# Loading batch 1's q and k ahead of WC1 and placing its first attention steps among batch 0's token steps, with one token-major q,k buffer

## The chip, the cores and the metric

The kernel runs on one core of a Trainium2 chip. The metric is the device time of one execution in microseconds (us); less is better. Of several executions the median is given. A profile is one execution, recorded instruction by instruction; its span runs from the first to the last instruction.

## The reference

What is computed is an attention with a sliding window and a linear bias, followed by an MLP mixer:

```
scores = q @ k^T / sqrt(64);  allowed where 0 <= i - j < 128
attn   = softmax(scores - slope[h] * |i - j|)            # slope[h] = 2 ** -(h + 1)
x      = attn @ v, heads side by side                    # (8, 576, 512)
u      = x + (relu(x^T @ w_tok1) @ w_tok2)^T             # mixing over 576 tokens, 256 hidden
out    = u + relu(u @ w_ch1) @ w_ch2                     # mixing over 512 channels, 1536 hidden
```

There are 8 batches, 8 heads, 576 tokens and a head dimension of 64. Inputs and output are float32; the kernel works in bfloat16 with float32 sums.

## The kernel before, in words

All work is in one program; every engine carries out its own instructions in the order in which they stand in its queue. Heads go in pairs, and a pair of a batch has a number `g`: batch 0 has pairs 0 to 3, batch 1 has 4 to 7, and so on. For each pair there are these steps:

- `regroup` (L139): two DVE copies, one for q and one for k, that bring the raw loads `qn`, `kn` into token-major order, `qg`, `kg`. It is done for a whole batch (in batch 0 for each pair). The raw tiles and the regrouped tiles have two buffers each, by `b % 2`.
- `att_T` (L193): twelve PE transposes of `qg`, `kg` into a PSUM tile `tT`, then a copy of q's half by ACT (L211, `qT`) and of k's half by DVE (L212, `kT`). In batch 0 ACT does both. `qT` and `kT` have four buffers each.
- `att_S` (L214), twice per pair: the score matmuls into `sp` (L230), two exponentials by ACT into `pe` (L238), a multiplication with the mask by DVE into `pb` (L242).
- `att_V` (L248): the matmuls of `pb` with v into `ot` (L264), then reciprocal and multiplication by DVE into `xb` (L271, L272). After the last pair of a batch it issues the loads of v two batches on.

The tiles `tT`, `sp` and `ot` share two PSUM buffers (`ps_at`); all PSUM tiles of the mixer share four (`ps_ma`).

The mixer of a batch goes in these steps: `tok1` twice (L304, matmuls at L307, a relu by ACT at L312), `tok2` five times (L315, matmuls at L320, addition of `xb` into `ub` by DVE at L324), `trans_u` four times (L328, PE transposes at L333 and L337, DVE copy into `UT` at L342), `ch1` 24 times (L344, four matmuls at L348, relu by ACT into `R2` at L353), and `ch2` for four or five chunks in three parts each (L357, matmuls at L376, addition of `ub` by DVE at L388 and a store by SyncE). `mixer_items` (L394) makes a list of these steps for batch `b` with the `ch2` chunks of batch `b - 1` among them, and `spread` (L17) mixes such a list with a list of attention steps, by the costs that are written beside them.

The first block of the body (L434) fixes the order on every engine as written: constants, loads, attention of batch 0, token steps of batch 0, and then `ch1` of batch 0 and the first two `ch2` chunks, mixed with the attention of batch 1. In the second block (L522) only PE's order is fixed as written, and a scheduler orders the other engines.

All loads are issued by POOL (GpSimd), because they convert to bfloat16. They go round eight semaphores, so a load can be issued only when the eighth load before it has landed. In the order of the queue they are: q,k of batch 0 by pairs (L450), v of batch 0, W1 and W2 for the token steps, WC1 in three parts (L463), q,k of batch 1 (L466), WC2 (L467), v of batch 1 (L470 to L472), then q,k of batch 2 (L492), v of batch 2, q,k of batch 3 (L513), and so on. The two iotas from which masks and identity are made (L441, L445) stand behind the first pair of loads.

The regroup of batch 1 stands ahead of batch 1's attention (L511), those of batches 2 and 3 at L517 and L524, and those of batches 4 to 7 in the `ch1` steps of `mixer_items` three batches earlier (L424, L425).

Of the kernel before, what the change touches and what calls it, by code (L numbers as in the profile page):

```python
# [13 lines left out]
TPP = 6  # L14
# [24 lines left out]
def kernel(  # L39
# [11 lines left out]
    nc = tc.nc  # L51
    P = nc.NUM_PARTITIONS
    B, H, S, D = q.shape
# [22 lines left out]

    const = ctx.enter_context(tc.tile_pool(name="const", bufs=1))
    pepool = ctx.enter_context(tc.tile_pool(name="pe", bufs=3))
    pbpool = ctx.enter_context(tc.tile_pool(name="pb", bufs=8))
    xpool = ctx.enter_context(tc.tile_pool(name="xp", bufs=2))  # L80
    rpool = ctx.enter_context(tc.tile_pool(name="rp", bufs=2))
    spool = ctx.enter_context(tc.tile_pool(name="sm", bufs=3))
    upool = ctx.enter_context(tc.tile_pool(name="up", bufs=2))
    opool = ctx.enter_context(tc.tile_pool(name="op", bufs=3))
    ps_at = ctx.enter_context(tc.tile_pool(name="ps_at", bufs=2, space=bass.MemoryType.PSUM))
    ps_ma = ctx.enter_context(tc.tile_pool(name="ps_ma", bufs=4, space=bass.MemoryType.PSUM))


    qn = [const.tile([P, H, TPP * D], bf16, name=f"qn{i}") for i in range(2)]
    kn = [const.tile([P, H, TPP * D], bf16, name=f"kn{i}") for i in range(2)]  # L90
    qg = [const.tile([P, TPP, H, D], bf16, name=f"qg{i}") for i in range(2)]
    kg = [const.tile([P, TPP, H, D], bf16, name=f"kg{i}") for i in range(2)]
    vp = [const.tile([P, NCH, H, D + 1], bf16, name=f"vp{i}") for i in range(2)]
    NR = 4
    qT = [const.tile([P, S], bf16, name=f"qT{i}") for i in range(NR)]
# [43 lines left out]
    def regroup(b, h0, h1, which=(0, 1)):  # L139

        for n in which:
            raw, t = ((qn, qg), (kn, kg))[n]
            nc.vector.tensor_copy(  # L143
                out=t[b % 2][:RP, :, h0:h1, :],
                in_=raw[b % 2][:RP, h0:h1, :].rearrange("p h (j d) -> p j h d", j=TPP),
            )

# [45 lines left out]
    def att_T(g, early=False):  # L193
        b, hp = divmod(g, NHP)
        if early:
            tt = [ps_ma.tile([P, 1024], bf16, name="tT1", tag="ma") for _ in range(2)]
        else:
            t2 = ps_at.tile([P, 2, 1024], bf16, name="tT", tag="at")
            tt = [t2[:, n, :] for n in range(2)]
        for n, t_raw in ((0, qg), (1, kg)):  # L200
            for j in range(TPP):
                nc.tensor.transpose(  # L202
                    tt[n][:, j * RP : (j + 1) * RP],
                    t_raw[b % 2][:RP, j, 2 * hp : 2 * hp + 2, :].rearrange("p h d -> p (h d)"),
                    ident[:RP, :RP],
                )
        def nat(n):
            return tt[n][:, 0:S].rearrange("c (j p) -> c p j", j=TPP)
        def dst(a):
            return a[:, :].rearrange("c (p j) -> c p j", j=TPP)  # L210
        nc.scalar.copy(out=dst(qT[g % NR]), in_=nat(0))  # L211
        (nc.scalar.copy if early else nc.vector.tensor_copy)(out=dst(kT[g % NR]), in_=nat(1))  # L212

    def att_S(g, half):  # L214
        b, hp = divmod(g, NHP)
# [178 lines left out]
    def mixer_items(b, lead=1):  # L394

        chunks = []
        if b > 0:
            cs = list(range(NF)) if (b - 1) % 2 == 0 else [NF] + list(range(NF))
            chunks = [ch2_items(b - 1, c) for c in cs]
        its = []  # L400
        for _ in range(lead if chunks else 0):
            its += chunks.pop(0)
        if b < B:
            its += [(1.07, lambda dh=dh: tok1(b, dh)) for dh in range(NDH)]
            if chunks:
                its += chunks.pop(0)
            mid = chunks.pop(0) if chunks else []
            for c in range(NCH):
                its.append((0.43, lambda c=c: tok2(b, c)))
                if mid and c % 2 == 0:  # L410
                    its.append(mid.pop(0))
            its += mid
            last = chunks.pop() if chunks else []
            for ch in chunks:
                its += ch
            its += last[:1]
            for cb in range(NCB):
                its.append((0.25, lambda cb=cb: trans_u(b, cb)))
            its += last[1:]
            for ht_i in range(NHT):  # L420
                for x in range(2):
                    its.append((0.48, lambda ht_i=ht_i, x=x: ch1(b, ht_i, x)))

                if ht_i in (4, 7) and 0 < b < B - 3:  # L424
                    its.append((0.0, lambda n=ht_i // 7: regroup(b + 3, 0, H, (n,))))  # L425
                if ht_i == 7 and 0 < b < B - 5:
                    its.append((0.0, lambda: dma_qk(b + 5, 0, H)))
        else:
            for ch in chunks:
                its += ch  # L430
        return its


    with tc.manual_schedule():  # L434
        for i in range(2):
            nc.vector.memset(vp[i][:, :, :, D : D + 1], 1.0)
            nc.vector.memset(vp[i][0 : P - TAIL, NF, :, 0:D], 0.0)
        nc.vector.memset(W1[0 : P - TAIL, NF, :], 0.0)
        nc.vector.memset(patT[0 : P - TAIL, :], 0.0)
        dma_qk(0, 0, 2)  # L440
        nc.gpsimd.iota(  # L441
            row[:, :], pattern=[[1, P]], base=0, channel_multiplier=0,
            allow_small_or_imprecise_dtypes=True,
        )
        nc.gpsimd.iota(  # L445
            pidx, pattern=[[0, 1]], base=0, channel_multiplier=1,
            allow_small_or_imprecise_dtypes=True,
        )
        for hp in range(1, NHP):
            dma_qk(0, 2 * hp, 2 * hp + 2)  # L450
        dma_v_tail(0)
        for h in range(H):
            dma_v_head(0, h)
        nc.gpsimd.dma_start(
            out=W1[:, 0:NF, :], in_=moe_w_tok1[0 : NF * P, :].rearrange("(c p) d -> p c d", p=P)
        )
        nc.gpsimd.dma_start(out=W1[P - TAIL : P, NF, :], in_=moe_w_tok1[NF * P : S, :])
        nc.gpsimd.dma_start(
            out=W2[:, :, :], in_=moe_w_tok2.rearrange("(j p) s -> p j s", p=P)
        )  # L460
        for n in range(3):
            cs = slice(n * DCH // 3, (n + 1) * DCH // 3)
            nc.gpsimd.dma_start(  # L463
                out=WC1[:, :, cs], in_=moe_w_ch1[:, cs].rearrange("(j p) h -> p j h", p=P)
            )
        dma_qk(1, 0, H)  # L466
        nc.gpsimd.dma_start(  # L467
            out=WC2[:, :, :], in_=moe_w_ch2.rearrange("(j p) c -> p j c", p=P)
        )
        dma_v_tail(1)  # L470
        for c in range(NF):
            dma_v(1, c)  # L472


        build_consts()
        regroup(0, 0, 2)
        build_bias()
        att_T(0, True)
        build_masks(0)
        regroup(0, 2, 4)  # L480
        att_S(0, 0)
        att_T(1, True)
        build_masks(1)
        att_S(0, 1)
        regroup(0, 4, 6)
        att_S(1, 0)
        att_T(2, True)
        build_masks(2)
        att_S(1, 1)
        regroup(0, 6, 8)  # L490
        if B > 2:
            dma_qk(2, 0, H)  # L492
        att_S(2, 0)
        att_T(3, True)
        build_masks(3)
        att_S(2, 1)
        att_V(0)
        att_S(3, 0)
        att_V(1)
        att_S(3, 1)  # L500
        att_V(2)
        att_V(3)
        nc.vector.tensor_copy(out=swap[:, 0:TAIL], in_=ident[:, TAIL:P])
        nc.vector.tensor_copy(out=swap[:, TAIL:P], in_=ident[:, 0:TAIL])


        its0, its1 = mixer_items(0), mixer_items(1, lead=2)
        n0, n1 = len(its0) - NHT, 6
        for _, f in its0[:n0]:
            f()  # L510
        side = [(0.0, lambda: regroup(1, 0, H))]  # L511
        if B > 3:
            side.append((0.0, lambda: dma_qk(3, 0, H)))  # L513
        for g in range(NHP - 2, 2 * NHP):
            side += att_step(g, NHP, 2 * NHP, outputs=False)
        side += [(0.6, lambda g=g: att_V(g)) for g in range(NHP, 2 * NHP)]
        side.append((0.0, lambda: regroup(2, 0, H)))  # L517
        if B > 4:
            side.append((0.0, lambda: dma_qk(4, 0, H)))
        spread(its0[n0:] + its1[:n1], side)  # L520

    with tc.manual_schedule(engines={ENG.PE}):  # L522
        side = att_step(2 * NHP - 2, 2 * NHP) + att_step(2 * NHP - 1, 2 * NHP)
        side.append((0.0, lambda: regroup(3, 0, H)))  # L524
        if B > 5:
            side.append((0.0, lambda: dma_qk(5, 0, H)))
        for g in range(2 * NHP, 3 * NHP):
            side += att_step(g)
        spread(its1[n1:], side)
        for b in range(2, B + 1):  # L530
            side = []
            for g in range(NHP * (b + 1), NHP * (b + 2)):
                side += att_step(g)
            spread(mixer_items(b), side)
# [30 lines left out]
```

## Time and profile before

| | us |
|---|---|
| median of 3 runs | 346.29 |
| lowest and highest | 345.74, 346.75 |
| the profiled execution | 345.74 |
| its span | 343.9 |
| PE busy in it | 307.2 |
| DVE, ACT, POOL busy in it | 179.6, 178.1, 60.0 |

The profile page begins with busy times, as in the table, and then shows the span in 40 slices of 8.6 us with a digit for the busy tenths of each engine. PE is TensorE, PEld its weight loads, DVE VectorE, ACT ScalarE, POOL GpSimd, SP SyncE. Further views list the groups of instructions by source line, the chain of waits that ended last, the DMA issues with their time to landing, and for any stretch the instructions in order of time. In that last view a line gives start, duration, engine, source line, operation, output and inputs with their sizes, the number of instructions merged into the line, and in brackets the time for which the engine was idle before it, with the releaser. The releaser is inferred, so it can name an instruction that had been done long before.

### The profile page before, as it was taken

What the parts mean: (1) busy time and instruction counts of PE and PEld (TensorE: products, weight loads), DVE (VectorE), ACT (ScalarE), POOL (GpSimd) and SP (SyncE); (2) the same over time, 40 slices, a digit from 0 to 9 for tenths busy, and PEclk for the clock granted to TensorE, in tenths of its full rate; (3) what the DMA queues carried; (4) which work ended last, traced back from release to release, by engine and by line L of the source; (5) the groups of instructions that cost most, each with busy time, mean ns of one, the idle gap of its engine ahead of it and who ended that gap; (6) DMA issues with size and microseconds to landing.
All of it is one profiled execution on the core that took longest, in us unless ns stands there. A gap on an engine that the chain in (4) does not pass through costs nothing.

```text
span 343.9 us, 6706 instructions
## 1 busy us (share of the span) xinstructions
PE 307.2 (89%) x2816; PEld 187.7 (55%) x2816; DVE 179.6 (52%) x342; ACT 178.1 (52%) x373; POOL 60.0 (17%) x79
## 2 busy tenths in 40 slices
PE   3578893097989999999999999999999999999995
PEld 1353672043467645765577446764576456746742
DVE  6873540457885479334953396336733573335012
ACT  4851495042659643784378433855396437612800
POOL 8973150107010400022000400040000000000000
PEclk9999999579999999999999999999999999999999
DMA  7999999789937759119110902093000210011022
GB/s 98 127 175 204 199 166 145 110 142 101 165 60 114 48 84 193 40 8 94 48 45 2 99 32 93 0 64 71 31 32 2 61 61 32 2 61 63 0 63 92
DMA packets 59502, 27.76 MB, mean 81 GB/s; under 512 B 38672, under 2 KB 54864, under 8 KB 59472
## 3 DMA queue, kind: packets, MB, share of 16 engines
q0 software_dynamic: 54224, 17.90, 53.2%
q1 hardware_dynamic: 5248, 9.44, 8.1%
q8 instruction: 22, 0.36, 0.5%
q14 instruction: 8, 0.07, 0.1%
HBM read 35.78 MB, written 9.44 MB: 131 GB/s over the span
## 4 chain that ended last, share of the span: by engine, by line
PE 77%; DMA 11%; DVE 6%; POOL 3%; ACT 2%; issue 1%; POOLq 0%; DVEq 0%
PE ct L348 25%; DMA qn_85<-in_q_dram 5%; PE sp L230 5%; PE ht L320 5%; PE ot L264 4%; DMA kn_88<-in_k_dram 4%; PE tT L202 3%; DVE xb L272 2%; PE ut L337 1%; DMA vp_93<-in_v_dram 1%; ACT pe L238 1%; POOL vp_93 L134 1%; PE o_782 L376 1%; POOL qn_85 L116 1%; PE o_2170 L376 1%
## 5 line engine op out<-in xcount | busy, mean ns | idle before, releaser
L348 PE MATMUL ct<-UT,WC_107 128*128 128x288 bf16 x768 | 104.8, 286 | 1.3 <-DVE UT L342 0.9
L238 ACT ACTIVATE pe<-sp,biascol 128x512 bf16<-128x512 f32 x128 | 81.5, 700 | 37.5 <-PE sp L230 36.1
L353 ACT ACTIVATE R_104<-ct 128x288 bf16<-128x288 f32 x192 | 73.8, 424 | 34.1 <-PE ct L348 27.9
L348 PEld LDWEIGHTS <-WC_107 128*128 128x128 bf16 x768 | 71.3, 98 | 23.6 <-issue 4.9
L242 DVE TENSOR_TENSOR pb<-pe,masks 128x1024 bf16<-128x1024 bf16 x64 | 44.1, 689 | 62.3 <-ACT pe L238 62.1
L376 PEld LDWEIGHTS <-R_104 128*128 128x128 bf16 x432 | 39.4, 98 | 42.2 <-issue 2.8
L324 DVE TENSOR_TENSOR ub<-ht,xb 128x512 bf16<-128x512 f32 x40 | 26.1, 681 | 6.7 <-PE ht L320 6.6
L128 POOL DMA_DIRECT2D vp_94<-in_v_dram x16 | 14.8, 937 | 71.0 <-PE ot L264 64.8
L264 PEld LDWEIGHTS <-pb 128*128 128x128 bf16 x576 | 23.0, 102 | 7.2 <-DVE xb L272 3.1
L272 DVE TENSOR_TENSOR xb<-ot,rt 128x640 bf16<-128x640 f32 x32 | 26.3, 823 | 1.0
L320 PE MATMUL ht<-r1t,W_106 128*128 128x512 bf16 x80 | 21.5, 383 | 0.3 <-ACT r1t L312 0.3
L128 POOL DMA_DIRECT2D vp_93<-in_v_dram x12 | 10.5, 891 | 53.6 <-PE ot L264 45.8
L230 PE MATMUL sp<-qT_97,kT_101 64*128 64x256 bf16 (+2 forms) x80 | 6.9, 273 | 13.7 <-DVE kT_102 L212 13.4
L264 PE MATMUL ot<-vp_93,pb 128*128 128x65 bf16 x288 | 13.2, 206 | 1.8 <-DVE xb L272 1.7
L307 PEld LDWEIGHTS <-W_105 128*128 128x128 bf16 x80 | 7.9, 103 | 12.7 <-issue 5.9
L211 ACT COPY qT_98<-tT 128x576 bf16<-128x576 bf16 x7 | 4.6, 660 | 19.4 <-PE tT L202 19.4
L342 DVE COPY UT<-ut 128x576 bf16<-128x576 bf16 x32 | 12.8, 447 | 1.6 <-PE ut L337 1.5
L230 PEld LDWEIGHTS <-kT_101 64*128 64x128 bf16 x80 | 2.9, 98 | 19.5 <-issue 18.6
L211 ACT COPY qT_95<-tT 128x576 bf16<-128x576 bf16 x7 | 4.5, 638 | 17.5 <-PE tT L202 17.3
L202 PEld LDWEIGHTS <-qg_89 96*128 96x128 bf16 x96 | 6.0, 106 | 12.1 <-DVE qg_89 L143 10.4
L320 PEld LDWEIGHTS <-W_106 128*128 128x128 bf16 x80 | 7.3, 99 | 9.4 <-issue 1.9
L212 DVE COPY kT_101<-tT 128x576 bf16<-128x576 bf16 x7 | 5.3, 756 | 12.8 <-ACT qT_97 L211 12.6
(190 smaller groups left out, 383.7 us busy)
## 6 DMA issues: line engine op xcount, KB each, us to landing
out_dram<-obt SPq DMA_DIRECT2D x32, 256.0 KB, 2.0
qn_86<-in_q_dram POOLq DMA_DIRECT2D x4, 576.0 KB, 9.6
kn_88<-in_k_dram POOLq DMA_DIRECT2D x4, 576.0 KB, 11.0
vp_94<-in_v_dram POOLq DMA_DIRECT2D x16, 128.0 KB, 4.8
qn_85<-in_q_dram POOLq DMA_DIRECT2D x3, 576.0 KB, 8.8
kn_87<-in_k_dram POOLq DMA_DIRECT2D x3, 576.0 KB, 11.6
WC_107<-in_moe_w_ch_dram POOLq DMA_DIRECT2D x3, 512.0 KB, 10.6
WC_108<-in_moe_w_ch_dram POOLq DMA_DIRECT2D x1, 1536.0 KB, 23.7
```

Of the source, the lines that this page charges most:

```text
L128: nc.gpsimd.dma_start(out=vp[b % 2][:, c, :, 0:D], in_=v[b, :, c * P : (c + 1) * P, :].rearrange("h s d -> s h d"),)
L202: nc.tensor.transpose(tt[n][:, j * RP : (j + 1) * RP], t_raw[b % 2][:RP, j, 2 * hp : 2 * hp + 2, :].rearrange("p h d -> p (h d)"), ident[: ...
L230: nc.tensor.matmul(sp[:, hh, i * 256 + x0 : i * 256 + x1], lhsT=kt[r, k0 : k0 + P], rhs=qt[r, q0 : q0 + x1 - x0], start=True, stop=True,)
L238: nc.scalar.activation(out=pe[:, i, :], in_=sp[:, i, :], func=ACT.Exp, bias=biascol[:, h : h + 1], scale=scale,)
L242: nc.vector.tensor_tensor(out=pb[:, :, :], in0=pe[:, :, :], in1=masks[:, half, 2 * hp : 2 * hp + 2, :], op=ALU.mult,)
L264: nc.tensor.matmul(ot[:, i, qb * (D + 1) : (qb + 1) * (D + 1)], lhsT=pb[:, i, col : col + P], rhs=vb[:, kc, h, :], start=(n == 0), stop=(n ...
L272: nc.vector.tensor_tensor(out=xb[b][:, :, 2 * hp * D : (2 * hp + 2) * D].rearrange("p c (i d) -> p i c d", i=2), in0=o4[:, :, :, 0:D], in1 ...
L320: nc.tensor.matmul(ht[:, :], lhsT=W2[:, j, c0(c) : c0(c) + P], rhs=r1s[b, j][:, :], start=(j == 0), stop=(j == NDH - 1),)
L324: nc.vector.tensor_tensor(out=ubs[b][:, c, :], in0=ht[:, :], in1=xb[b][:, c, :], op=ALU.add)
L348: nc.tensor.matmul(ct[:, :], lhsT=WC1[:, cb, ht_i * P : (ht_i + 1) * P], rhs=UT[:, cb, o : o + SH], start=(cb == 0), stop=(cb == NCB - 1),)
L353: nc.scalar.activation(out=R2[:, ht_i, o : o + SH], in_=ct[:, :], func=ACT.Relu)
L376: nc.tensor.matmul(o2[0][:, :], lhsT=R2[:, ht_i, col : col + P], rhs=WC2[:, ht_i, :], start=(ht_i == 0 and c != NF), stop=(ht_i == NHT - 1),)
```

## The change

- The raw loads of q,k of batch 1 are issued ahead of the three parts of WC1 in place of behind them.
- In batch 0, the regroup of batch 1 and `att_T` of pairs 4 and 5 stand behind `tok1`, and three of the four `att_S` of these pairs stand between the `tok2` and `trans_u` steps, the fourth behind `trans_u`. `att_T` and `att_S` of pairs 6 and 7 are spread over the 24 `ch1` steps, and the four `att_V` over the first six `ch2` parts.
- The token-major tiles `qg`, `kg` have one buffer each. The regroup of batch `b + 1` is now part of `att_T` of the last pair of batch `b`, for `b` from 1 to 6, followed by the load of q,k of batch `b + 3`. The regroups at L424, L517 and L524, and their loads, are gone.
- The iotas stand ahead of the first load. The two memsets of the second v tile are done by POOL, ahead of the v loads of batch 1, in place of by DVE at the start.
- `pb` has nine buffers in place of eight, the output tile `obt` four in place of three.

```diff
-    pbpool = ctx.enter_context(tc.tile_pool(name="pb", bufs=8))
+    pbpool = ctx.enter_context(tc.tile_pool(name="pb", bufs=9))
...
-    opool = ctx.enter_context(tc.tile_pool(name="op", bufs=3))
+    opool = ctx.enter_context(tc.tile_pool(name="op", bufs=4))
...
-    qg = [const.tile([P, TPP, H, D], bf16, name=f"qg{i}") for i in range(2)]
-    kg = [const.tile([P, TPP, H, D], bf16, name=f"kg{i}") for i in range(2)]
+    qg = const.tile([P, TPP, H, D], bf16, name="qg")
+    kg = const.tile([P, TPP, H, D], bf16, name="kg")
...
         (nc.scalar.copy if early else nc.vector.tensor_copy)(out=dst(kT[g % NR]), in_=nat(1))
+        if hp == NHP - 1 and 0 < b < B - 1:
+            regroup(b + 1, 0, H)
+            if b + 3 < B:
+                dma_qk(b + 3, 0, H)
...
-                if ht_i in (4, 7) and 0 < b < B - 3:
-                    its.append((0.0, lambda n=ht_i // 7: regroup(b + 3, 0, H, (n,))))
-                if ht_i == 7 and 0 < b < B - 5:
-                    its.append((0.0, lambda: dma_qk(b + 5, 0, H)))
...
-        for i in range(2):
-            nc.vector.memset(vp[i][:, :, :, D : D + 1], 1.0)
-            nc.vector.memset(vp[i][0 : P - TAIL, NF, :, 0:D], 0.0)
+        def v_consts(e, i):
+            e.memset(vp[i][:, :, :, D : D + 1], 1.0)
+            e.memset(vp[i][0 : P - TAIL, NF, :, 0:D], 0.0)
+
+        v_consts(nc.vector, 0)
         nc.vector.memset(W1[0 : P - TAIL, NF, :], 0.0)
         nc.vector.memset(patT[0 : P - TAIL, :], 0.0)
-        dma_qk(0, 0, 2)
         nc.gpsimd.iota(
...
-        for hp in range(1, NHP):
+        for hp in range(NHP):
             dma_qk(0, 2 * hp, 2 * hp + 2)
...
+        dma_qk(1, 0, H)
         for n in range(3):
             cs = slice(n * DCH // 3, (n + 1) * DCH // 3)
             nc.gpsimd.dma_start(
                 out=WC1[:, :, cs], in_=moe_w_ch1[:, cs].rearrange("(j p) h -> p j h", p=P)
             )
-        dma_qk(1, 0, H)
         nc.gpsimd.dma_start(
             out=WC2[:, :, :], in_=moe_w_ch2.rearrange("(j p) c -> p j c", p=P)
         )
+        v_consts(nc.gpsimd, 1)
         dma_v_tail(1)
...
-        n0, n1 = len(its0) - NHT, 6
-        for _, f in its0[:n0]:
+        its0 = [f for _, f in its0]
+        n1 = 6
+        t1, t2, ut, c1 = (
+            its0[:NDH], its0[NDH : NDH + NCH], its0[NDH + NCH : NDH + NCH + NCB],
+            its0[NDH + NCH + NCB :],
+        )
+        g = NHP
+        order = t1 + [
+            lambda: regroup(1, 0, H), lambda: att_T(g), lambda: att_T(g + 1),
+            t2[0], t2[1], lambda: att_S(g, 0), t2[2], t2[3], lambda: att_S(g, 1), t2[4],
+            lambda: att_S(g + 1, 0), *ut, lambda: att_S(g + 1, 1),
+        ]
+        if B > 3:
+            order.append(lambda: dma_qk(3, 0, H))
+        for f in order:
             f()
-        side = [(0.0, lambda: regroup(1, 0, H))]
-        if B > 3:
-            side.append((0.0, lambda: dma_qk(3, 0, H)))
-        for g in range(NHP - 2, 2 * NHP):
-            side += att_step(g, NHP, 2 * NHP, outputs=False)
-        side += [(0.6, lambda g=g: att_V(g)) for g in range(NHP, 2 * NHP)]
-        side.append((0.0, lambda: regroup(2, 0, H)))
-        if B > 4:
-            side.append((0.0, lambda: dma_qk(4, 0, H)))
-        spread(its0[n0:] + its1[:n1], side)
+        side = [(0.6, lambda: att_T(g + 2))]
+        side += [(0.5, lambda x=x: att_S(g + 2, x)) for x in range(2)]
+        side += [(0.6, lambda: att_T(g + 3))]
+        side += [(0.5, lambda x=x: att_S(g + 3, x)) for x in range(2)]
+        spread([(0.48, f) for f in c1], side)
+        spread(its1[:n1], [(0.6, lambda x=x: att_V(g + x)) for x in range(NHP)])
...
-        side.append((0.0, lambda: regroup(3, 0, H)))
-        if B > 5:
-            side.append((0.0, lambda: dma_qk(5, 0, H)))
```

More of the change, by code (lines that the diff above doesn't have):

```diff
@@ L143, in regroup @@
             nc.vector.tensor_copy(
-                out=t[b % 2][:RP, :, h0:h1, :],
+                out=t[:RP, :, h0:h1, :],
                 in_=raw[b % 2][:RP, h0:h1, :].rearrange("p h (j d) -> p j h d", j=TPP),
@@ L203, in att_T @@
                     tt[n][:, j * RP : (j + 1) * RP],
-                    t_raw[b % 2][:RP, j, 2 * hp : 2 * hp + 2, :].rearrange("p h d -> p (h d)"),
+                    t_raw[:RP, j, 2 * hp : 2 * hp + 2, :].rearrange("p h d -> p (h d)"),
                     ident[:RP, :RP],
```

## Prediction

> **What bounds the kernel now.** The page's first part gives PE 307.2 us of a 343.9 us span, so about 37 us are left in which PE does nothing. The second part shows where: the PE row has its low digits in the first third only, and from the twelfth slice on it reads 9. I therefore read PE in order of time, to see each gap and its releaser, then DVE over the largest gap, then POOL over what DVE waits for.
>
> The first view is PE's timeline (start, duration, instruction, and in brackets the idle time before it with its releaser):
>
> ```profile
> 31.54 0.63 PE L320 MATMUL ht<-r1t,W_106 128*128 128x512 bf16 x1
> 32.43 2.10 PE L320 MATMUL ht<-r1t,W_106 128*128 128x512 bf16 x9 [0.26 <-ACT r1t L312]
> 35.98 0.23 PE L333 MATMUL ut<-ident,ub 128*128 128x128 bf16 x1 [1.45 <-DVE ub L324]
> ...
> 68.42 0.61 PE L230 MATMUL sp<-qT_97,kT_101 64*128 64x256 bf16 x6 [13.43 <-DVE kT_102 L212]
> 68.96 1.89 PE L376 MATMUL o_782<-WC_108,R_104 128*128 128x512 bf16 x4
> ...
> 80.20 1.24 PE L307 MATMUL t_959<-xb,W_105 128*128 128x512 bf16 x5 [1.42 <-DVE xb L272]
> ...
> 82.70 0.43 PE L202 MATMUL tT<-ident,kg_91 96*128 96x96 bf16 x6 [0.81 <-DVE kg_91 L143]
> ...
> 97.42 1.38 PE L348 MATMUL ct<-UT,WC_107 128*128 128x288 bf16 x4 [0.94 <-DVE UT L342]
> ```
>
> One stall of 13.43 us stands ahead of 68.42. Four 512-column matmuls then take 1.89 us, where four others of line 376 take 1.03 us later: up to about 73.1 PE runs at half speed, which costs some 2.3 us more. After 97.42 PE shows one gap, 0.70 us at 245.37. So the time falls by what PE gains before 97, less what the change puts into the full part behind it.
>
> The second view is DVE's timeline over the stall:
>
> ```profile
> 63.81 0.96 DVE L143 COPY qg_90<-qn_86 96x3072 bf16<-96x3072 bf16 x1 [10.66 <-DMA qn_86<-in_q_dram]
> 64.69 0.68 DVE L242 TENSOR_TENSOR pb<-pe,masks 128x1024 bf16<-128x1024 bf16 x1
> 66.74 0.96 DVE L143 COPY kg_92<-kn_88 96x3072 bf16<-96x3072 bf16 x1 [1.37 <-DMA kn_88<-in_k_dram]
> 67.62 0.75 DVE L212 COPY kT_102<-tT 128x576 bf16<-128x576 bf16 x1
> ```
>
> This regroup is that of batch 3. It stands on DVE ahead of kT of pair 7, which PE needs, and waits for loads issued late:
>
> ```profile
> 19.09 0.82 POOL L116 DMA_DIRECT2D qn_86<-in_q_dram  x1
> 19.87 0.80 POOL L116 DMA_DIRECT2D kn_88<-in_k_dram  x1
> ...
> 36.64 0.77 POOL L116 DMA_DIRECT2D kn_87<-in_k_dram  x1 [2.07 <-DMA kn_88<-in_k_dram]
> ...
> 52.93 0.77 POOL L116 DMA_DIRECT2D kn_88<-in_k_dram  x1 [1.40 <-DMA qn_85<-in_q_dram]
> ```
>
> POOL's brackets also give landing times: the three WC1 parts at about 25.2, 28.0 and 31.2, q of batch 1 at 33.2 and its k at 36.1 (14.1 and 16.2 us after issue in the list of DMA issues), WC2 at 44.3, the last v part of batch 1 at 50.7, q of batch 2 at 52.4, its k at 55.7 (19.1 us after 36.64). They land in the order of issue, 2.5 to 3.2 us apart for these sizes.
>
> **Part 1: the loads.** q,k of batch 1 change places with WC1. Both are equal in kind: five transfers, WC1 512 KB each, q,k 576 KB each. Put ahead, q lands near 25.4 and k near 28.2, and WC1 near 30.8, 33.4 and 36.4; what follows (WC2, v of batch 1, q,k of batch 2) has the same bytes ahead and keeps its times. The regroup on DVE can start at 27.4 (the swap copies end there) and end at 29.2 to 30.0. First use is the end of the second tok1, 31.74: hidden, with 1.7 us to spare. WC1 is first used near 40.9 below: hidden, with more.
>
> **Part 2: the order of batch 0.** PE from 31.74, durations from warm rows: two att_T 0.51 each (to 32.8), tok2[0,1] 0.43 each. DVE has to do kT4, kT5 (0.67 apart), five ub adds (0.62), three pb (0.60), four UT copies (0.38): 8 us against PE's 6, so DVE sets this stage. ACT's qT4 ends at 33.0, so kT4 33.7, kT5 34.4, ub0 35.1, ub1 35.7, pb 36.4, ub2 37.0, ub3 37.7, pb 38.3, ub4 39.0. The transposes of u need ub4: PE idles from about 36.2 to 39.05, a 2.85 us gap where before there was 1.45. They end at 40.15, pb(5,0) and UT copies at 41.2, and the first ch1 ends at 41.4. Then 23 ch1 at 0.49, two att_T and four att_S at 0.33: ch1 ends at 55.0. ACT in the same stretch does 24 relus at 0.31, five exp pairs at 1.22 and two qT at 0.52, 14.6 us in all, just level. Then six ch2 parts (0.86) and four att_V (0.55), 7.4 us, to 62.4; reciprocal and xb of the last (1.2 with latency) let tok1 of batch 1 start at **63.75** instead of 80.20: **-16.45**. The stall with its half-speed time goes; the moved scores cost PE nothing new.
>
> **Part 3: regroup of batch 2.** It now stands behind kT7 (about 50.5) and ahead of the last two pb. It waits for k at 55.7; then kg, two pb, four reciprocal-xb pairs (1.0) and two ob adds (0.6) need some 7.5 us, ending 63.2. PE's own path ends at 63.75, so this is hidden by half a microsecond only. The 0.81 us at 82.70, which waited for this regroup, goes: **-0.8**.
>
> **Part 4: one buffer, later batches.** In the changed kernel's instruction order the regroup of batch 3 stands on DVE between kT of pair 11 and the UT copies; before, a regroup stood behind them, at 98.38. Those copies set PE's 0.94 us gap at 97.42, so the pair of copies (98.38 to 100.13 before) is paid in full: **+1.75**. At the next four batches it stands between the first ub add and the others, both halves ahead of kT (batches 4 and 6) or one (5 and 7), and must wait for the transposes of the same buffer. With those at 125.94 to 126.55 and 1.8 us of copies, the second ub add ends at 129.7, and the last tok2 (about 129.05) needs its PSUM buffer: +0.7; by the other order +0.4. Sum **+2.2**, between 0 (another buffer is free) and 1.8 each, 7.2 (no cover). I take the value nearest to the DVE rows at 125.58 to 129.14.
>
> On POOL's queue the loads of q,k of batch 4 now stand ahead of v of batch 3, and wait for the regroup of batch 2, until about 56.7. The v loads behind them wait for the last att_V of batch 1 in any case (62.4; 78.86 before), and each later q,k load likewise stands ahead of a v load whose release comes later. The first use of q,k of batch 4 is the regroup near 110, fifty microseconds on: 0.
>
> **Part 5: small edits.** The two iotas go ahead of the first load; they took POOL from 2.71 to 3.05, so the first load is 0 to 0.34 later, and DVE waited for it (0.46 us at 4.53): **+0.2**. The two memsets for v of batch 1 leave DVE, which then idled 0.73 us anyway: 0. On POOL, where they are not seen, they take between 0.1 (its own memset row) and an estimated 1 us (twice DVE's 0.48), ahead of v loads that have 5 us to spare: 0. The ninth pb and fourth ob buffers: no wait for either shows in DVE's brackets, 0.
>
> DVE's regroup took 1.34 us a copy at 80.06, beside POOL's issuing, against 0.95 at 98.38, hence the 30.0 above. [...]
>
> **Sum.** -16.45 - 0.8 + 1.75 + 2.2 + 0.2 = **-13.1 us**. The profiled execution took 345.74 us (343.9 of span and 1.84 around it): 332.6. The median of the runs is 0.55 above it, so I put the median at **333.2 us**.
>
> **The gap and the clock.** Gaps of 1.45 and 1.42 us left PE's speed alone, that of 13.43 us halved it for 4.7 us. The new gaps, 2.85 us ahead of u's transposes and 2.7 at the UT copies of batch 1, lie between. I take no loss, being nearer to the short ones, and keep 2.3 us for each as the other end. [...]
>
> **Rivals.**
> - **More gain (0.15).** The four later regroups find free buffers and the token stage is closer to PE's own work (27.1 us from 31.74, so tok1 near 62): -16.45 - 1.7 - 0.8 + 1.75 + 0.2 = -17, 329. For it: DVE had 0.2 to 3 us idle times between its groups after 100. Against it: DVE's rows from 124 to 133 show none.
> - **Clock lost or regroups bare (0.13).** Both gaps cost 2.3, or the four regroups 1.8 each: 5 us less gain, about 338. For it: PE is full there, so every delay counts.
> - **The load is no earlier (0.06).** If transfers share instead of queueing, k of batch 1 still lands at 36.1, att_T waits until 37.0, 5.2 us plus a cold clock: -7, 339.3. Against it: the landings in order of issue.
> - **Slower (0.05).** The wait moves to regroup of batch 2, on DVE ahead of the last two pb: tok1 starts 7.5 us after k of batch 2 lands. It costs from a landing of 56.2 on, one for one, and decides at 56.2 + 13.1 = 69.3; at 72 the time is 349. Against it: that k landed at 55.7 with the same bytes ahead.
>
> **How the numbers follow.** The forecast, 331 to 336, has 0.60; with a remainder of 0.01 for no change. A measurement tells 0.3% (1 us). Faster 0.94, same 0.01, slower 0.05. The range takes in the larger gain and most of the smaller ones: 328.0 to 339.5.
>
> **What would show it.** Right: the 13.43 us gap is gone; tok1 of batch 1 starts near 64; PE has a gap near 36 to 39; the ct gap of batch 1 is near 2.7 us; k of batch 1 lands near 28. Wrong: a DVE regroup with a long DMA wait ahead of it; half-speed matmuls after 40; PE gaps at ht of more than 1 us in each later batch.

## The result, and the profile after

The changed kernel takes 333.75 us (median of four runs, 332.32 to 334.71), the kernel before 346.52 us in the four runs set against it. The ratio is 0.9624, with a 95% interval from 0.9575 to 0.9673. The forecast was 333.2 us. The profiled execution took 334.71 us with a span of 332.9, 11.0 us less than the span before.

PE's timeline of the changed kernel answers to the first view of the kernel before (start, duration, instruction, number merged, idle time ahead with its releaser):

```profile
39.93 0.23 PE L337 MATMUL ut<-ident,ub 128*128 128x128 bf16 x1 [2.33 <-DVE ub L328]
...
57.06 0.66 PE L352 MATMUL ct<-UT,WC_105 128*128 128x288 bf16 x4
57.56 1.03 PE L380 MATMUL o_828<-WC_106,R_102 128*128 128x512 bf16 x4
...
66.31 1.24 PE L311 MATMUL t_957<-xb,W_103 128*128 128x512 bf16 x5 [1.22 <-DVE xb L276]
...
84.09 1.49 PE L352 MATMUL ct<-UT,WC_105 128*128 128x288 bf16 x4 [2.67 <-DVE UT L346]
85.52 0.61 PE L234 MATMUL sp<-qT_95,kT_99 64*128 64x256 bf16 x4
86.06 2.10 PE L352 MATMUL ct<-UT,WC_105 128*128 128x288 bf16 x8
...
117.59 0.59 PE L324 MATMUL ht<-r1t,W_104 128*128 128x512 bf16 x2 [0.33 <-DVE ub L328]
```

The gap of 13.43 us is gone, and `tok1` of batch 1 starts at 66.31 in place of 80.20. Between 40 and 65 PE has no other gap, and the 1.22 us ahead of `tok1` stand where 1.42 stood before. New are the 2.33 us ahead of the transposes of u, the 2.67 us ahead of batch 1's `ch1`, and small ones at `ht`. Behind the 2.67 us gap eight `ct` matmuls take 2.10 us, where eight at 88.50 take 1.15: PE runs there at half speed, with a granted clock of 0.50 over 85 to 88.

DVE's timeline of the changed kernel, over the place of the former stall and over the UT copies:

```profile
53.16 0.76 DVE L212 COPY kT_100<-tT 128x576 bf16<-128x576 bf16 x1 [1.25 <-ACT qT_96 L211]
53.83 0.95 DVE L143 COPY qg<-qn_85 96x3072 bf16<-96x3072 bf16 x1
55.04 0.96 DVE L143 COPY kg<-kn_87 96x3072 bf16<-96x3072 bf16 x1 [0.26 <-DMA kn_87<-in_k_dram]
56.08 0.69 DVE L246 TENSOR_TENSOR pb<-pe,masks 128x1024 bf16<-128x1024 bf16 x1
...
81.19 0.74 DVE L212 COPY kT_100<-tT 128x576 bf16<-128x576 bf16 x1
81.86 0.95 DVE L143 COPY qg<-qn_86 96x3072 bf16<-96x3072 bf16 x1
82.72 0.95 DVE L143 COPY kg<-kn_88 96x3072 bf16<-96x3072 bf16 x1
83.59 1.54 DVE L346 COPY UT<-ut 128x576 bf16<-128x576 bf16 x4
```

The regroup behind kT of pair 7 is now that of batch 2, whose k has just landed: DVE waits 0.26 us for it. The regroup of batch 3 stands ahead of the UT copies and holds them for 1.73 us.

POOL's timeline shows the loads of batch 1, and through POOL's waits when they land:

```profile
16.00 0.83 POOL L116 DMA_DIRECT2D qn_86<-in_q_dram  x1
16.79 0.92 POOL L116 DMA_DIRECT2D kn_88<-in_k_dram  x1
...
24.93 0.88 POOL L128 DMA_DIRECT2D vp_92<-in_v_dram  x1 [1.26 <-DMA qn_86<-in_q_dram]
28.87 1.60 POOL L128 DMA_DIRECT2D vp_92<-in_v_dram  x1 [3.07 <-DMA kn_88<-in_k_dram]
```

q has landed by 24.9 and k by 28.9, ahead of the copies of the regroup, which start on DVE at 28.17 and 29.04 without a wait, and of the first transposes at 32.36.

### The profile page after: what moved, and what is told of

It reads as the page before. It is cut to its first block, busy times and chain, and to the rows that moved or that the text cites. A ratio compares the mean times of both kernels' runs of the same rounds, so it can differ in the third digit from the quotient of the medians.

```text
span 332.9 us, 6713 instructions
## 1 busy us (share of the span) xinstructions
PE 307.6 (92%) x2816; PEld 189.1 (57%) x2816; DVE 178.9 (54%) x340; ACT 178.5 (54%) x373; POOL 60.9 (18%) x81
## 4 chain that ended last, share of the span: by engine, by line
PE 82%; DVE 11%; issue 2%; ACT 2%; DMA 2%; POOL 1%; POOLq 0%
PE ct L352 30%; PE sp L234 5%; PE ot L268 5%; PE tT L202 4%; PE ht L324 3%; DVE ub L328 2%; PE ut L341 2%; DVE kg L143 2%; DMA kn_87<-in_k_dram 2%; DVE pb L246 1%; ACT pe L242 1%; DVE qg L143 1%; DVE kT_100 L212 1%; DVE xb L276 1%; PE o_3667 L380 1%
## 5 line engine op out<-in xcount | busy, mean ns | idle before, releaser
L352 PE MATMUL ct<-UT,WC_105 128*128 128x288 bf16 x768 | 106.0, 290 | 2.8 <-DVE UT L346 2.7
L357 ACT ACTIVATE R_102<-ct 128x288 bf16<-128x288 f32 x192 | 72.7, 422 | 30.4 <-PE ct L352 24.7
L202 PEld LDWEIGHTS <-qg 96*128 96x128 bf16 x192 | 12.4, 105 | 14.8 <-DVE qg L143 10.1
L202 PE MATMUL tT<-ident,qg 96*128 96x96 bf16 x168 | 12.2, 210 | 0.0
L202 PE MATMUL tT<-ident,kg 96*128 96x96 bf16 x168 | 12.0, 209 | 0.0
```

What stands on the lines that cost most here:

```text
L202: nc.tensor.transpose(tt[n][:, j * RP : (j + 1) * RP], t_raw[:RP, j, 2 * hp : 2 * hp + 2, :].rearrange("p h d -> p (h d)"), ident[:RP, :RP],)
L352: nc.tensor.matmul(ct[:, :], lhsT=WC1[:, cb, ht_i * P : (ht_i + 1) * P], rhs=UT[:, cb, o : o + SH], start=(cb == 0), stop=(cb == NCB - 1),)
L357: nc.scalar.activation(out=R2[:, ht_i, o : o + SH], in_=ct[:, :], func=ACT.Relu)
```

## The experiments

Two theories were set against each other. **A**: the time was lost in one stall, a regroup that stood on DVE ahead of kT of pair 7 and waited for a late load, and the change is faster because its order has that regroup elsewhere. **B**: the gain comes from the early load of batch 1 and from its scores standing among the token steps. The experiments form three groups, e1 to e4, e5 to e8 and e9 to e11. In each group the kernel before ran beside them on the same chip (medians 345.04, 344.72 and 345.24 us), and the ratios are to that.

**One regroup moved, in the kernel before** (e1_regroup3_last):

```diff
             side.append((0.0, lambda: dma_qk(4, 0, H)))
+        side.append((0.0, lambda: regroup(3, 0, H)))
+        if B > 5:
+            side.append((0.0, lambda: dma_qk(5, 0, H)))
         spread(its0[n0:] + its1[:n1], side)
...
-        side.append((0.0, lambda: regroup(3, 0, H)))
-        if B > 5:
-            side.append((0.0, lambda: dma_qk(5, 0, H)))
```

> The kernel before with one edit: the regroup of batch 3 and the load behind it are issued as the last thing of the first block, so DVE does them behind the regroup of batch 2. Theory A (the gain is the end of one stall, a regroup that stood ahead of kT of pair 7): the 13.43 us gap goes, tok1 of batch 1 starts near 65 to 67 instead of 80.2, time 331.5 to 334.5. Theory B (the gain comes from the early load of batch 1 and the scores among the token steps): at most 2 us faster, 344 to 347, with the gap still over 10 us.

Measured: 330.97 us, ratio 0.9619 (0.9583 to 0.9655). PE's timeline of this kernel:

```profile
55.92 0.40 PE L230 MATMUL sp<-qT,kT 64*128 64x256 bf16 x6 [0.87 <-DVE kT L212]
...
65.54 1.24 PE L307 MATMUL t<-xb,W 128*128 128x512 bf16 x4 [1.42 <-DVE xb L272]
...
82.68 1.38 PE L348 MATMUL ct<-UT,WC 128*128 128x288 bf16 x4 [0.94 <-DVE UT L342]
```

The 13.43 us are 0.87, and `tok1` of batch 1 starts at 65.54, as early as in the changed kernel. An edit that moves one pair of copies, with the load behind them, gives the whole gain of the change. Theory A holds (the time lies half a microsecond below its range); B's 344 to 347 is missed by 13 us.

**The early load alone, in the kernel before** (e2_loads_only): the two lines that load q,k of batch 1 stand ahead of WC1.

```diff
+        dma_qk(1, 0, H)
         for n in range(3):
...
-        dma_qk(1, 0, H)
         nc.gpsimd.dma_start(
             out=WC2[:, :, :], ...
```

> The kernel before with q,k of batch 1 loaded ahead of WC1 and nothing else. Theory A: the stall waits for k of batch 3, which has the same bytes ahead of it, so 345.5 to 347.5 and a gap of 12 to 14.5 us ahead of kT of pair 7. Theory B: 336 to 343.

Measured: 344.91 us, ratio 1.0005 (0.998 to 1.0029): nothing. That is 0.6 us below the range of theory A and far from that of B. PE's gap is 12.43 us. DVE's timeline shows the same regroup of batch 3 in its old place:

```profile
63.28 0.96 DVE L143 COPY qg<-qn 96x3072 bf16<-96x3072 bf16 x1 [9.65 <-DMA qn<-in_q_dram]
64.16 0.68 DVE L242 TENSOR_TENSOR pb<-pe,masks 128x1024 bf16<-128x1024 bf16 x1
66.22 0.96 DVE L143 COPY kg<-kn 96x3072 bf16<-96x3072 bf16 x1 [1.38 <-DMA kn<-in_k_dram]
```

**The changed kernel with the old order of batch 0** (e3_old_order): early loads, one buffer and the regroups in `att_T` are kept; `att_T`, `att_S` and `att_V` of batch 1 go back among `ch1` and `ch2`.

```diff
-        order = t1 + [ lambda: regroup(1, 0, H), lambda: att_T(g), ... ]
-        for f in order:
-            f()
...
+        for _, f in its0[:n0]:
+            f()
+        side = [(0.0, lambda: regroup(1, 0, H))]
+        if B > 3:
+            side.append((0.0, lambda: dma_qk(3, 0, H)))
+        for g in range(NHP - 2, 2 * NHP):
+            side += att_step(g, NHP, 2 * NHP, outputs=False)
+        side += [(0.6, lambda g=g: att_V(g)) for g in range(NHP, 2 * NHP)]
+        spread(its0[n0:] + its1[:n1], side)
```

> The changed kernel with the order of batch 0 as before (all of batch 1's attention among ch1 and ch2), early loads, one buffer and regroups in att_T kept. Theory A: no long stall, tok1 of batch 1 near 65 to 67 as in the changed kernel, 332 to 335.5. Theory B: the scores among the token steps are worth most of the gain, 339 or more.

Measured: 334.09 us, ratio 0.9688 (0.9655 to 0.9721), `tok1` of batch 1 at 65.39. The interval overlaps that of the changed kernel in the second group (0.9614 to 0.9684), so the placement among the token steps is worth little in this form.

**The changed kernel with the late load** (e4_late_load):

```diff
-        dma_qk(1, 0, H)
         for n in range(3):
...
+        dma_qk(1, 0, H)
         nc.gpsimd.dma_start(
             out=WC2[:, :, :], ...
```

> The changed kernel with q,k of batch 1 loaded behind WC1 as before. My price of the rival: k lands at 36 to 37, the regroup ends near 37.5, att_T of pair 4 starts about 5 us late, tok1 of batch 1 near 71 to 72, 338 to 341. If the early load is not needed by the new order: 333 to 335.

Measured: 339.53 us, ratio 0.9869 (0.9819 to 0.992). PE's timeline:

```profile
34.20 0.66 PE L202 MATMUL tT<-ident,qg 96*128 96x96 bf16 x6 [2.88 <-DVE qg L143]
37.08 0.66 PE L202 MATMUL tT<-ident,kg 96*128 96x96 bf16 x6 [2.21 <-DVE kg L143]
...
70.39 1.24 PE L311 MATMUL t<-xb,W 128*128 128x512 bf16 x5 [1.22 <-DVE xb L276]
```

Behind these two gaps PE is slow as well: four `ht` matmuls take 1.91 us at 38.50 and 1.04 at 40.84, and the granted clock is 0.50 over 38 to 40 and 0.82 over 40 to 42. The early load brings nothing by itself (e2), but the new order needs it: without it 1.3% of gain are left of the 3.5 to 3.8% of the changed kernel, so nearly two thirds are gone. The two are one edit.

The other experiments start from the changed kernel, which ran again beside the next three (e5_changed_again).

> The changed kernel itself, beside the next three on one chip: 332.3 to 334.7 as in its four runs. If the half-speed stretches behind the two PE gaps (2.3 and 2.7 us) are not the same in every execution, its times spread by 1 to 2.5 us more than those of a kernel without the gaps.

Measured: 333.09 us (331.54 to 334.95), ratio 0.9649 (0.9614 to 0.9684). The times spread over 3.4 us, those of e1, which has neither gap, over 1.6 (six and four executions).

**Two token-major buffers again** (e6_two_buffers; `pb` and `obt` go back to eight and three for the space):

```diff
-    qg = const.tile([P, TPP, H, D], bf16, name="qg")
-    kg = const.tile([P, TPP, H, D], bf16, name="kg")
+    qg = [const.tile([P, TPP, H, D], bf16, name=f"qg{i}") for i in range(2)]
+    kg = [const.tile([P, TPP, H, D], bf16, name=f"kg{i}") for i in range(2)]
...
-                out=t[:RP, :, h0:h1, :],
+                out=t[b % 2][:RP, :, h0:h1, :],
...
-                    t_raw[:RP, j, ...],
+                    t_raw[b % 2][:RP, j, ...],
```

> The changed kernel with two token-major q,k buffers again (and eight pb, three ob buffers for space). The instruction order then has the regroup of batch 3 ahead of kT of pair 7 once more. Theory A (that place is the stall, and the one buffer is what forbids it): a PE gap of 8 to 13 us there, 341 to 346. Theory B (one buffer or two makes no difference beside the early loads): 331 to 334.

Measured: 346.4 us, ratio 1.0043 (1.0023 to 1.0063): the whole gain is gone, and the time and the gap lie slightly above the ranges of theory A. DVE's timeline:

```profile
64.00 0.96 DVE L143 COPY qg<-qn 96x3072 bf16<-96x3072 bf16 x1 [12.59 <-DMA qn<-in_q_dram]
66.38 0.96 DVE L143 COPY kg<-kn 96x3072 bf16<-96x3072 bf16 x1 [1.42 <-DMA kn<-in_k_dram]
67.26 0.75 DVE L212 COPY kT<-tT 128x576 bf16<-128x576 bf16 x1
67.92 0.95 DVE L143 COPY qg<-qn 96x3072 bf16<-96x3072 bf16 x1
```

PE's gap ahead of pair 7's scores is 14.14 us. The regroup of batch 3 is written in `att_T` of pair 11 here too, yet with a free buffer the scheduler put it ahead of kT of pair 7 on DVE. With one buffer it must follow pair 11's transposes, and cannot go there. So the single buffer does the work of an order, and the gain hangs on this part of the change. That the smaller `pb` and `obt` are not to blame is seen in e10 below, which has them too. The single buffer alone, in the kernel before, was not run.

**Regroup of batch 3 behind the UT copies** (e7_regroup3_behind_UT):

```diff
-        if hp == NHP - 1 and 0 < b < B - 1:
+        if hp == NHP - 1 and 0 < b < B - 1 and b != 2:
...
-        spread(its1[n1:], side)
+        main = its1[n1:]
+        k1 = len(main) - 2 * NHT + 1
+        spread(main[:k1] + [(0.0, late_regroup)] + main[k1:], side)     # regroup(3), dma_qk(5)
```

> The changed kernel with the regroup of batch 3 behind the first ch1 step of batch 1, so that DVE makes the UT copies first. If those two copies are paid in full and the 2.67 us gap costs PE its full clock: the gap falls to about 0.9 us (-1.75) and the ct and sp matmuls behind it run at full speed (-1.3), together -3, so 329.5 to 331.5 where the changed kernel has 333. If the clock is lost for another reason: -1.75 only, half-speed ct stay.

Measured: 329.66 us, ratio 0.9551 (0.9522 to 0.9581), 3.4 us below the changed kernel. PE's timeline:

```profile
38.42 0.23 PE L337 MATMUL ut<-ident,ub 128*128 128x128 bf16 x1 [2.33 <-DVE ub L328]
38.48 0.39 PE L341 MATMUL ut<-ident,ub 128*128 128x128 bf16 x4
...
79.45 1.38 PE L352 MATMUL ct<-UT,WC 128*128 128x288 bf16 x4 [0.94 <-DVE UT L346]
80.76 0.39 PE L234 MATMUL sp<-qT,kT 64*128 64x256 bf16 x4
81.08 1.15 PE L352 MATMUL ct<-UT,WC 128*128 128x288 bf16 x8
```

The gap is 0.94 us again and what follows runs at full speed, with a granted clock of 1.00 over 80 to 90: both the wait and the clock are paid for by the gap, as the first alternative has it. In this execution the other gap, still 2.33 us, did not cost the clock: the transposes behind it take 0.39 us, and its mean clock is 1.0. Of its six times three are 328.68 to 328.88, all at clock 1.0, and three 330.44 to 330.63, all at 0.995.

**A filler in the gap of the token stage** (e8_filler): ten matmuls whose result nobody reads.

```diff
-            lambda: att_S(g + 1, 0), *ut, lambda: att_S(g + 1, 1),
+            lambda: att_S(g + 1, 0), filler, *ut, lambda: att_S(g + 1, 1),
...
+            ft = ps_ma.tile([P, DM], f32, name="ft", tag="ma")
+            for _ in range(10):
+                nc.tensor.matmul(ft[:, :], lhsT=W2[:, 0, 0:P], rhs=r1s[0, 0][:, :], start=True, stop=True)
```

> The changed kernel with ten unread 512-column matmuls on PE ahead of the transposes of u in batch 0, about 2.2 us of work in the 2.33 us gap; nothing else is added. If the gap costs the clock: the transposes, sp and ct behind it run at full speed, -0.8 to -1.5 us. If the half-speed stretch there has another cause: no gain, or up to 0.5 us slower.

Measured: 332.76 us, ratio 0.9635 (0.9608 to 0.9661). In the profile the transposes behind the filler take 0.39 us for four, as in e7 at a clock of 1.00, and the mean clock is 0.992 to 0.995 in all six executions, which is one half-speed stretch (that behind the 2.67 us gap) where the changed kernel mostly has two. Against 333.09 the gain of 0.3 us is within the intervals, though: unclear in time.

**The filler with the regroup of batch 3 moved** (e9_filler_and_late_regroup3, the last two diffs together):

> The kernel with the regroup of batch 3 behind the UT copies, plus the ten unread matmuls in the gap of batch 0's token stage. That kernel's six times without the filler fell into two groups, 328.7 to 328.9 at a mean granted clock of 1.0 and 330.4 to 330.6 at 0.995. If the 2.33 us gap is what decides between them: all executions in the lower group, median 328.5 to 329.2, clock 1.0. If the clock is lost elsewhere: two groups again.

Measured: 329.94 us, ratio 0.9542 (0.9515 to 0.9568). The clock was 0.998 to 1.0 in all five executions, as expected, but the times still fell into two groups, 328.5 to 328.7 and 329.9 to 330.2. That expectation was missed. In the profiled execution (329.94) PE came to full speed late, before the gap: the first transposes of batch 1 at 32.11 take 0.69 us for six, where the last kernel below takes 0.42 at 32.18. From `tok1` of batch 0 to that of batch 1 this execution takes 36.78 us, where the one profiled for e7 takes 35.84. So the start has a spread of its own, which hides a filler's gain here.

**Two buffers, with the order set by hand** (e10_two_buffers_placed, from e6_two_buffers): the regroup of batch 3 is the last thing of the first block, the later ones stand in `att_T` of each batch's second pair.

```diff
-        if hp == NHP - 1 and 0 < b < B - 1:
+        if hp == (NHP - 1 if b == 1 else 1) and 0 < b < B - 1 and b != 2:
...
         spread(its1[:n1], [(0.6, lambda x=x: att_V(g + x)) for x in range(NHP)])
+        regroup(3, 0, H)
+        if B > 5:
+            dma_qk(5, 0, H)
```

> The changed kernel with two token-major buffers (eight pb, three ob buffers), the regroup of batch 3 issued as the last thing of the first block and the later ones during the batch before the transposes that need them. It should have neither the 13 us stall nor the UT gap nor the ht gaps (0.33, 0.40, 0.33), but one wait of up to 1.5 us where the regroup of batch 3 meets its load (k at 65 to 67) ahead of kT of pair 8: 328 to 330.5, two groups 1.8 apart. If the stall returns in another place: 333 or more.

Measured: 329.89 us, ratio 0.9548 (0.9521 to 0.9575). Behind 66 PE has two gaps, 0.94 us ahead of `ct` and 0.70 at 229.53, both as in the kernel before; the regroup of batch 3 waits 0.45 us for its load; the gaps at `ht` are gone. Five of six executions lie at 329.57 to 330.93 with clocks of 0.993 and 0.995, one at 328.32 with 1.0.

**The same with the filler** (e11_two_buffers_placed_filler):

> The same with the ten unread matmuls in the token stage's gap: the lower group of the kernel without them in every execution, 328 to 329.5.

Measured: 328.6 us (328.4 to 329.0), ratio 0.9517 (0.9494 to 0.9541), clock 0.998 or 0.999 throughout. Here the filler is seen: all four executions lie beside the fastest of the kernel without it, 1.3 us below its median, though the intervals of the two ratios overlap. It is the fastest of the study, some 4.5 us below the changed kernel; without useless work, e7_regroup3_behind_UT and e10_two_buffers_placed are 3 to 3.5 us below it.

## Why the prediction was right, step by step

The forecast of 333.2 against 333.75 is better than its parts, and some of that is luck. The sum was worked out for the profiled execution of the kernel before, the fastest of its four, and between the two profiled executions it missed by 2.1 us; that of the changed kernel is the slowest of its four. Two terms were too hopeful, the first and the clock; the later regroups and, by less, the second were too dark. Beside each term of the sum stands the change of the distance between the same instructions in the two profiled executions.

| step | forecast | measured | from |
|---|---|---|---|
| start to `tok1` of batch 1, with the start's 0.2 | -16.25 | -13.89 | 80.20 and 66.31 |
| the wait for batch 2's regroup | -0.8 | -1.18 | on to `o`, 84.56 and 69.49 |
| regroup of batch 3 ahead of the UT copies | +1.75 | +1.74 | on to `ct`, 97.42 and 84.09 |
| clock behind that gap | 0 | +1.37 | on to `ot`, 101.46 and 89.50 |
| regroups of batches 4 to 7 | +2.2 | +0.93 | on to the last `ch2`, 337.66 and 326.63 |
| sum | -13.1 | -11.03 | |

**The stall** was read rightly: its place, that it ends, and that nothing as long follows. e1, e2 and e6 show it from three sides. The text had the cause in "This regroup is that of batch 3. It stands on DVE ahead of kT of pair 7", but then credited the 16.45 us to the order of batch 0. Part 4 has the new place of that regroup, but only as a cost of 1.75. e1 has the same gain without that order. What the rest of the change adds is seen between e1 (0.9619) and e7 (0.9551), both free of the longer UT gap: some 2 us. Between e3 and the changed kernel it cannot be told from nothing, and the profiled executions show why. From `tok1` of batch 0 to that of batch 1 the old order takes 37.58 us (e3), the new one 35.84 where PE kept its clock (e7) and 37.94 where it did not (e5, which also came to full speed later): what the new order gains there, the clock takes.

**The loads** (part 1) landed as worked out, q 24.9 and k 28.8 against 25.4 and 28.2. (The 2.5 to 3.2 us between landings are not quite what its own times give, which is 2.0 to 3.3; nothing rested on it.) The rival "the load is no earlier" was priced at 339.3, 7 us below the kernel before; e4 measured 339.53, 5.5 below it on its chip.

**Part 2** failed by 2.4 us in that execution. The gap was forecast at 2.85 and is 2.33, and `ch1` ended at 57.6 in place of 55.0. (By its own terms, 62.4 and 1.2, `tok1` would start at 63.6 and not at 63.75.) The start was later by 0.82 us (`tok1` at 28.14 against 27.32). That cannot be put down to the iotas: with the iotas in the old place the kernels e1 and e2 have `tok1` at 27.39 and 28.22, and with them ahead it lies between 27.54 and 28.33. The rest is the clock. e7 has the same instructions up to there, kept the clock in its profiled execution (1.00 over 38 to 48) and takes 35.84 us from `tok1` of batch 0 to that of batch 1; the forecast has 36.43, the changed kernel 38.17. So the path itself was right within 0.6 us.

**The clock** is the step that failed: "I take no loss, being nearer to the short ones". The view by stages of the changed kernel (the stage and its length, busy time of PE, PEld, DVE, ACT and POOL, then the granted clock, the DMA share and GB/s) shows it:

```profile
39.00:40.00 1.00, 0.07 (x2) 0.08 (x3) 1.00 (x3) 0.20 (x1) 0.00 (x0) 1.00 1.31 225
40.00:41.00 1.00, 1.00 (x16) 1.00 (x17) 1.00 (x3) 0.00 (x0) 0.00 (x0) 0.76 1.19 195
41.00:42.00 1.00, 1.00 (x11) 0.74 (x11) 0.92 (x3) 0.00 (x0) 0.00 (x0) 0.50 1.42 191
42.00:43.00 1.00, 1.00 (x10) 0.54 (x7) 0.23 (x1) 0.68 (x2) 0.00 (x0) 0.50 2.17 163
43.00:44.00 1.00, 1.00 (x6) 0.65 (x5) 0.38 (x1) 0.89 (x3) 0.00 (x0) 0.53 3.26 143
44.00:45.00 1.00, 1.00 (x18) 0.88 (x17) 0.31 (x1) 0.69 (x2) 0.64 (x1) 1.00 3.57 141
```

PE is fully busy from 40 on, but the clock is at half from 40.5 to 43.9. The same happens from 84.9 to 88.3. Over the ten executions of the changed kernel the mean clock is 0.99 in seven (332.7 to 335.0 us) and 0.995 in three (331.5 to 332.3); in none is it 1.0. One stretch of 3.4 us at half speed lowers the mean by 0.005, so this reads as both stretches in seven and one in three; only two of the seven were profiled, and they have both. The other end of the price, 2.3 us each, was too high. Behind the second gap the table has 1.37. For the first, e10 with the stretch and e11 without, which come to full speed nearly alike, take 37.25 and 35.92 us from `tok1` to `tok1`: 1.3 us.

**The later regroups** cost less than forecast. The gaps are 0.33, 0.40 and 0.33, at batches 4, 5 and 6 (0.55, 0.40 and 0.55 in the executions profiled for e5 and e7), against 0.7, 0.4 and 0.7 (and 0.4); the wait was for the second `ub` addition as described, but some of it had slack. The 0.93 is a net figure: a gap of 0.70 us that the kernel before had at 245.37 is gone, so that the rest of this stretch costs 1.6. Of that, 1.06 is in the three gaps; where the remainder lies is open.

**Part 3** held: k of batch 2 landed at 55.0, and the wait was 0.26 us. The rival that was slower than before did not come near its point of 69.3.

## What to carry to other kernels

When an in-order engine waits long for a load, ask first whether the waiting instruction stands in the right place: here moving one pair of copies gave as much as the whole change, and loading other data earlier gave nothing. A second buffer can cost time, because it frees a scheduler to put a copy where its load has not landed (here 346.4 us with two against 333.09 with one); if two buffers are wanted, fix the order by hand. Price a new PE gap with the slow matmuls behind it too: here gaps of 2.33 and 2.67 us cost about 1.3 us above their length in most executions, while those of 1.45 and 1.42 us in the kernel before left the granted clock at 1.00.

## What the runs showed of the hardware

The clock fell after gaps shorter than expected, and not in every execution. In the changed kernel, in steps of 0.1 us, the granted clock falls and rises twice (columns as above):

```profile
40.50:40.60 0.10, 0.10 (x5) 0.10 (x3) 0.10 (x1) 0.00 (x0) 0.00 (x0) 0.61 1.29 215
43.90:44.00 0.10, 0.10 (x2) 0.10 (x1) 0.10 (x1) 0.00 (x0) 0.00 (x0) 0.82 3.64 128
...
84.80:84.90 0.10, 0.08 (x1) 0.08 (x1) 0.10 (x1) 0.00 (x0) 0.01 (x1) 0.98 0.66 69
88.30:88.40 0.10, 0.10 (x4) 0.04 (x4) 0.00 (x0) 0.10 (x1) 0.00 (x0) 0.95 1.33 207
```

A clock of 0.61 over 0.1 us means that it fell from 1.0 to 0.5 after 0.02 us. So it is at half from 40.52 to 43.94 and from 84.90 to 88.31, for 3.4 us each time, and falls 0.6 and 0.8 us after PE has begun to work again. In e10 it reads 0.74 over 38 to 40. Had it fallen only when PE began again at 39.41, that would be 0.85, so there it fell inside the gap. Gaps of the same length read thus:

| execution | PE idle | length | granted clock behind it |
|---|---|---|---|
| changed kernel | 37.60 to 39.93 | 2.33 | 0.50 from 40.52 to 43.94 |
| changed kernel | 81.42 to 84.09 | 2.67 | 0.50 from 84.90 to 88.31 |
| e10 | 37.08 to 39.41 | 2.33 | 0.50 over 40 to 42 |
| e8 | 79.77 to 82.44 | 2.67 | 0.50 over 84 to 86 |
| e7 | 36.09 to 38.42 | 2.33 | 1.00 over 38 to 48 |
| e3 | 80.49 to 83.16 | 2.67 | 1.00 over 82 to 90 |
| e4 | 43.07 to 45.40 | 2.33 | 1.00 over 44 to 48 |

So a gap of 2.33 us cost the clock in two of these executions and not in two others, and one of 2.67 us in two and not in a third. The length alone does not decide it, and what does is not shown here. In the kernel before, the gaps of 1.45 and 1.42 us left the clock at 1.00 (over 34 to 40 and 78 to 86).

The start spreads as well. In the changed kernel, e7, e9, e10 and e11, whose instructions are the same up to there but for the q,k buffers of e10 and e11, `tok1` of batch 0 begins between 27.57 and 28.33 us. No edit of this study explains that. PE also comes to full speed at different times: the first transposes of batch 1 take 0.69 us for six at 32.36 in the changed kernel and 0.42 at 32.33 in e10. In the changed kernel sixes of transposes take 0.60 us at 33.32 and 0.42 at 33.76; in e9 they take 0.46 at 33.07 and 0.42 at 33.37. The granted clock reads 1.00 over 32 to 34 in all three, so the mean clock does not contain the slow start.
